# Softcap attention with a max-out layer behind it: a fourth step of the attention loop inverts its sums on chip, reciprocals are spread before the transposing DMA, turned reciprocals get buffers of their own, and GpSimd takes five of six weight differences

## The chip, the core and the metric

One core of a Trainium2 chip runs the whole kernel. TensorE (PE) multiplies matrices; VectorE (DVE), ScalarE (ACT) and GpSimd (POOL) do elementwise work; SyncE (SP) issues most of the DMAs, in program order, as does each engine with its own instructions. Matrix products land in PSUM, everything else on chip lies in SBUF. The metric is device time in microseconds (us), median over runs, from launch to end of one execution.

## The reference

`q`, `k`, `v` are 8 batches of 12 heads of 448 rows of 64; the weights `w1`, `w2` are 768x1024 and `w_out` is 1024x768.

```python
scores = scale * np.matmul(q, k.transpose(0, 1, 3, 2))
scores = cap * np.tanh(scores / cap)
scores = scores - np.max(scores, axis=-1, keepdims=True)
attn = np.exp(scores)
attn = attn / (np.sum(attn, axis=-1, keepdims=True) + 1e-09)
attn_out = np.matmul(attn, v)
...
x = attn_out.transpose(0, 2, 1, 3).reshape(B * S, H * D)
g = np.maximum(x @ w1, x @ w2)
out = g @ w_out
```

## The kernel before

**Algebra.** Since max(a, b) = b + relu(a - b), the kernel forms `wd = w1 - w2` (six slices of 128 rows, `subtract(c)`, L217) and `wm = w2 @ w_out` (`turn_w2`, `premultiply`) once, and then out = relu(x wd) w_out + x wm. No row maximum is taken, because tanh bounds the scores; the sum of the exponentials divides at the end.

**Steps.** Heads are handled in pairs, 48 of them; one step `t` (0 to 23) of the attention loop takes two pairs, `ab` = 0 and 1. Six pairs, or three steps, make one batch. Loads, casts and crossbar transposes go in groups `g` of three pairs: `load` (SP), `cast` (mostly GpSimd, to bf16), then for g >= 2 `cross(g)` (L271), a transposing DMA that writes `qkT`, which the score matmuls read. A step makes scores in four parts (L298, L293), ScalarE takes tanh (L299, L301) and exp (L306) of each, PE multiplies with the values (L341, L344; tile `pv`), and VectorE adds the exponentials up in `esum` (L325, L327, L329), so that few matmuls with ones give the row sums (`ss`). The score parts of step t+1 are issued during step t.

**Two ways to invert the sums.** Steps in the tuple `CHIP` (L513) do it on chip: `turn` transposes the sums in 32x32 blocks on VectorE (L385), `unturn` takes the reciprocal of one column (L389) and transposes it back (L391); for steps from 3 on (`chip_late`) GpSimd then multiplies pair 0 (L435) and VectorE pair 1 straight from PSUM (L438). All other steps go through DRAM: VectorE copies sums (L366) and values (L350), a DMA packs the sums (L368), VectorE inverts (`invert`, L396) in the next step, a DMA writes them out (L398), two DMAs broadcast them to all partitions (`spread`, L404, tile `rec_b`) in the step after that, and GpSimd multiplies both pairs (`normalize`, L418). Both ways write `xT`, the x of the reference.

**Filler.** The max-out layer of a batch (`moe(b)`: L455 multiplies by `wd`, L459 takes the relu, L467 and L470 multiply by `wm` and `w_out`, L474 copies out) is a queue of single matmuls, of which `F(n)` puts the next n between the matmuls of the attention. moe(0) is queued at the end of step 2, moe(1) at step 6, moe(2) at 9, moe(3) at 12, moe(4) at 17, and so on. So the order on PE is fixed by the program, and a matmul that waits holds up all behind it, scores too. What is left of the filler runs behind the attention loop.

**Order on the other queues.** In step t of the loop SP is given `cross(crosses[t])` (steps 4, 5, 7, 8, 10, 11, 13, 14, 16, 17, 19, 20), then `spread(t - 2)` where step t-2 is not in `CHIP`, then the loads; `normalize(t - 2)` is queued on GpSimd in the middle of the step.

**Buffers.** A pool hands out the buffers of a name in turn, and a new user waits until all readers of the old one are through: `tn` has two, shared by the turned sums and the turned reciprocals, `rec_b` has one, `w2T` three, `qkT` two.

Of the kernel before, what the change touches and what calls it, by code (L numbers as in the profile page):

```python
# [10 lines left out]
def kernel(  # L11
# [12 lines left out]
    f32 = mybir.dt.float32  # L24
    bf16 = mybir.dt.bfloat16
# [3 lines left out]
    B, H, S, D = q.shape  # L29
# [3 lines left out]
    P = 128  # L33
    KC, FC = DM // P, DF // P
# [13 lines left out]
    stage = ctx.enter_context(tc.tile_pool(name="stage", bufs=2))  # L48
    att = ctx.enter_context(tc.tile_pool(name="att", bufs=2))
    upool = ctx.enter_context(tc.tile_pool(name="upool", bufs=2))  # L50
    xpool = ctx.enter_context(tc.tile_pool(name="xpool", bufs=2))
# [164 lines left out]
    def subtract(c, eng=nc.vector):  # L216
        eng.tensor_sub(wd_sb[:, c, :], w1_in[c], w2b[:, c, :])  # L217

    w2T = {}

    def turn_w2(c):
        ps = mm_psum.tile([P, 512], f32, name="mm").bitcast(bf16)
        for f in range(FC):
            nc.tensor.transpose(ps[:, f * P : (f + 1) * P], w2b[:, c, f * P : (f + 1) * P], ident)
            yield
        w2T[c] = stage.tile([P, FC * P], bf16, name="w2T", bufs=3)
        nc.vector.tensor_copy(w2T[c], ps)

    def premultiply(c):
# [39 lines left out]
    def cross(g):  # L269

        nc.sync.dma_start_transpose(  # L271
            out=qkT_of(g).rearrange("p n j c -> p (n j) c"), in_=kqf[g % 2].rearrange("p n j c -> p (n j c)")
        )
# [6 lines left out]
    def scores(t, p, m0=0, m1=2):  # L280

        if m0 == 0:
            tanh[t, p] = att.tile([P, 4, S], bf16, name="tanh")
        if p == 2:
            s = s_psum.tile([P, 2, 512], f32, name="s")
        for m, (ab, j) in list(enumerate(PARTS[p]))[m0:m1]:
            i = 2 * t + ab
            g = i // L
            k0 = qkT[g][:, i % L, :, :].rearrange("p j c -> p (j c)")
            o = Q0 + (64 * (i // NP % 2) if g >= NT else 0)  # L290
            qTn = k0[:, o : o + S]
            if p == 2:
                nc.tensor.matmul(s[:, m, :S], k0[:, 3 * P : 4 * P], qTn)  # L293
                continue
            s = s_psum.tile([P, 2, 512], f32, name="s")
            for h in range(2):
                r = slice(64 * h, 64 * h + 64)
                nc.tensor.matmul(s[:, h, :S], k0[r, j * P : (j + 1) * P], qTn[r, :])  # L298
            nc.scalar.activation(tanh[t, p][:, 2 * m : 2 * m + 2, :], s[:, :, :S], AF.Tanh, scale=scale / cap)  # L299
        if p == 2:  # L300
            nc.scalar.activation(tanh[t, p][:, 0:2, :], s[:, :, :S], AF.Tanh, scale=scale / cap)  # L301

    def ex(t, p):
        n = 2 if p == 2 else 4
        expo[t, p] = att.tile([P, n, S], bf16, name=f"expo{p}", bufs=1 if p == 3 else 2)
        nc.scalar.activation(expo[t, p], tanh[t, p][:, 0:n, :], AF.Exp, scale=float(cap))  # L306

    def e_of(t, ab, j):
        p, m = LP[ab, j]
        return expo[t, p][:, m : m + (1 if j == NJ else 2), :]  # L310
# [20 lines left out]
    U, sums, rec, recd = {}, {}, {}, {}  # L331
    HALF = [slice(64 * h, 64 * h + 64) for h in range(2)]
    NB = S // 32
# [13 lines left out]
    def keep(t, ab, ps):  # L347
        if ab == 0:
            U[t] = upool.tile([P, 2, S], f32, name="u", bufs=3)
        nc.vector.tensor_copy(U[t][:, ab, :], ps[:, :S])  # L350
# [19 lines left out]
    turned = {}  # L370

    def turn(t, ab):

        ss = pv_psum.tile([P, 512], f32, name="ss")
        if t < NS:
            for j in range(NJ):
                for h in range(2):
                    nc.tensor.matmul(ss[HALF[h], :S], ones, e_of(t, ab, j)[:, h, :], start=(j == 0), stop=False)
            for h in range(2):
                nc.tensor.matmul(ss[HALF[h], :S], ones2[:, h, :], expo[t, 2][:, ab, :], start=False, stop=True)  # L380
        else:
            for h in range(2):
                nc.tensor.matmul(ss[HALF[h], :S], ones, esum[t][:, 2 * ab + h, :], start=True, stop=True)
        st = turned[t, ab] = upool.tile([P, NB, 32], f32, name="tn", bufs=2)
        nc.vector.transpose(st.rearrange("p b c -> p (b c)"), ss[:, :S])  # L385

    def unturn(t, ab):
        rs = upool.tile([P, NB, 1], f32, name="rs", bufs=2)
        nc.vector.reciprocal(rs, turned[t, ab][:, :, 0:1])  # L389
        rb = upool.tile([P, S], f32, name="tn", bufs=2)  # L390
        nc.vector.transpose(rb.rearrange("p (b c) -> p b c", c=32), rs.to_broadcast([P, NB, 32]))  # L391
        return rb

# [4 lines left out]
        nc.sync.dma_start(out=recd[t], in_=r)  # L398

    def spread(t):  # L400
        rec[t] = xpool.tile([P, 2, S], f32, name="rec_b", bufs=1)
        lines = recd[t].rearrange("(n h a) c -> h n (a c)", h=2, a=8)
        for h in range(2):
            nc.sync.dma_start(  # L404
                out=rec[t][64 * h : 64 * h + 64, :, :], in_=lines[h : h + 1, :, :].to_broadcast([64, 2, S])
            )
# [9 lines left out]
    def normalize(t):  # L416
        for ab in range(2):
            nc.gpsimd.tensor_mul(x_of(t, ab), U[t][:, ab, :], rec[t][:, ab, :])  # L418

    def chip(t, ab):  # L420
        turn(t, ab)
        ps = values(t, ab)
        yield
        rb = unturn(t, ab)
        yield
        nc.vector.tensor_mul(x_of(t, ab), ps[:, :S], rb)
# [13 lines left out]
    def run(parts, n=2):  # L440
        for _ in parts:
            F(n)
# [56 lines left out]
    def F(n):  # L499
        rate[1] += n * rate[0]  # L500
        while rate[1] >= 1 and fill_q:
            try:
                next(fill_q[0])
                rate[1] -= 1
            except StopIteration:
                fill_q.pop(0)
        if not fill_q:
            rate[1] = 0.0
# [1 line left out]

    NL = N // L
    NS = 3
    CHIP = (0, 1, 2, 4, 5, 8, 11)  # L513
    todo = [[] for _ in range(N)]
    crosses = {}

# [42 lines left out]
    for _ in turn_w2(0):  # L559
        pass  # L560
# [34 lines left out]
    def extra(i):  # L595
        for f, a in todo[i]:
            f(*a)
# [6 lines left out]
    for _ in turn_w2(1):  # L604
        pass
# [22 lines left out]
    for t in range(1, 3):  # L628
        scores(t + 1, 0)
        ex(t, 3)  # L630
        F(6)
        if t == 2:
            subtract(0)
        run(chip(t, 0), 5)
        if t == 2:
            for c in range(1, 5):
                subtract(c, nc.gpsimd)
            cast(nc.gpsimd, 3, "k")
            cast(nc.gpsimd, 3, "q")
            cross(3)  # L640
        F(6)
        scores(t + 1, 1)
        ex(t + 1, 0)
        F(6)
        run(chip(t, 1), 5)
        if t == 2:
            subtract(5)
            cast(nc.gpsimd, 2, "v")
            load(3, "v")
            fill_q.append(moe(0))  # L650
        scores(t + 1, 2)
        ex(t + 1, 1)
        F(10)
        if t == 2:
            extra(4)
            extra(5)
        scores(t + 1, 3)
        ex(t + 1, 2)
        F(8)
    add(3, 0, 0)  # L660

    for t in range(3, NQ):
        i = 2 * t
        more = t + 1 < NQ
        if t % 3 == 0 and 3 < t < 13 or t % 3 == 2 and t > 16:
            fill_q.append(moe(t // 3 - 1))
        if more:
            scores(t + 1, 0)
        ex(t, 3)
        F(2)  # L670
        add(t, 0, 1)
        F(6 if more else 2)
        if t in crosses:
            cross(crosses[t])
        if t > 4 and t - 2 not in CHIP:
            spread(t - 2)
        if t == 3:
            cast(nc.gpsimd, 3, "v")
        extra(i)
        F(5 if more else 3)  # L680
        if more:
            scores(t + 1, 1)
            ex(t + 1, 0)
        keep(t, 0, values(t, 0))
        F(4)
        add(t, 1, 0)
        F(6 if more else 4)
        if t > 4 and t - 2 not in CHIP:
            normalize(t - 2)
        if more:  # L690
            scores(t + 1, 2)
            ex(t + 1, 1)
        add(t, 0, 2)
        F(2)
        add(t, 1, 2)
        F(4 if more else 3)
        add(t, 1, 1)
        F(2 if more else 8)
        if t > 3 and t - 1 not in CHIP:
            invert(t - 1)  # L700
        extra(i + 1)
        F(2 if more else 0)
        if more:
            scores(t + 1, 3)
            ex(t + 1, 2)
        if t in CHIP:
            run(chip_late(t), 1)
        else:
            keep(t, 1, values(t, 1))
            total(t)  # L710
            F(3)
        F(1)
        if more:
            add(t + 1, 0, 0)
        F(3 if more else 0)
    F(6)
    spread(NQ - 2)
    F(10)
    invert(NQ - 1)
# [40 lines left out]
```

## Time and profile before

| what | value |
|---|---|
| median of 7 runs | 378.62 us |
| lowest, highest | 376.97, 382.16 us |
| the profiled execution | 381.26 us, of which the span is 379.5 us |
| PE busy | 348.1 us (92% of the span) |
| ScalarE busy | 281.5 us (74%) |
| VectorE busy | 247.7 us (65%) |
| GpSimd busy | 158.5 us (42%) |
| mean granted TensorE clock | 0.976 of full |

The span runs from the first instruction to the last; the 1.76 us between span and time lie around it. A timeline line gives the start, the duration, the engine, the line of the code, the operation, its output and input, a count, and in brackets the idle time ahead of it with what ended it. A line of the chain of waits gives start, duration and what the chain passed through. ScalarE works until 311.5 us; behind that only filler is left on PE.

### The profile page before, as it was taken

To read this page: it belongs to the slowest core of one execution; us is meant where nothing else is said; L and a number is where in the kernel's file an instruction comes from. 1 tells how busy PE (TensorE), PEld (TensorE's weight loads), DVE (VectorE), ACT (ScalarE), POOL (GpSimd) and SP (SyncE) were. 2 spreads that over 40 slices of the span, in tenths; PEclk is the share of its full clock that TensorE was granted. 3 is DMA by queue.
4 is the path that set the end of the run, shared out by engine and by line. 5 is a ranking of instruction groups with operands and counts; after the bars stand their busy time and mean duration, and the time that the engine had idled before them with its cause. 6 is when DMAs were issued, how large, how long until landed. Compare 5 with 4: busy or idle time off the path is not lost.

```text
span 379.5 us, 6115 instructions
## 1 busy us (share of the span) xinstructions
PE 348.1 (92%) x2278; PEld 165.9 (44%) x2278; DVE 247.7 (65%) x413; ACT 281.5 (74%) x265; POOL 158.5 (42%) x193
## 2 busy tenths in 40 slices
PE   4679988999599998899999999999999899999996
PEld 2335543444134443244444444444444345555553
DVE  4237647868747667877879758688676878433521
ACT  4993678999949997699999999999999892000000
POOL 6635782703374136611692266427734232220000
PEclk9899999999879998899999999999999999999999
DMA  7999969672984499387894987797985032322022
GB/s 254 260 224 301 328 190 245 197 197 63 261 259 89 127 255 287 118 153 206 259 257 149 265 251 212 207 286 208 206 222 159 2 92 92 115 95 99 2 83 85
DMA packets 109523, 69.80 MB, mean 184 GB/s; under 512 B 64308, under 2 KB 104500, under 8 KB 109492
## 3 DMA queue, kind: packets, MB, share of 16 engines
q1 hardware_dynamic: 107540, 66.25, 62.4%
q0 software_dynamic: 1952, 3.15, 4.5%
q8 instruction: 18, 0.29, 0.3%
q14 instruction: 13, 0.11, 0.1%
HBM read 50.27 MB, written 11.13 MB: 162 GB/s over the span
## 4 chain that ended last, share of the span: by engine, by line
PE 34%; ACT 30%; DMA 12%; SPq 8%; POOL 6%; issue 5%; DVE 5%; POOLq 0%; DVEq 0%; ACTq 0%
ACT expo L306 14%; ACT tanh L299 13%; PE mm L455 11%; PE mm L470 9%; PE mm L467 7%; DMA qr<-in_q_dram 5%; PE pv L341 3%; DMA vr<-in_v_dram 3%; DMA kr<-in_k_dram 2%; DMA rec_b<-rec_d 2%; PE s L298 2%; SPq L271 2%; ACT tanh L301 2%; SPq L131 2%; POOL xT L418 1%
## 5 line engine op out<-in xcount | busy, mean ns | idle before, releaser
L299 ACT ACTIVATE tanh<-s 128x896 bf16<-128x896 f32 x144 | 124.2, 914 | 29.9 <-PE s L298 28.1
L306 ACT ACTIVATE expo<-tanh 128x1792 bf16<-128x1792 bf16 (+1 forms) x96 | 144.8, 1509 | 0.1
L470 PE MATMUL mm<-wo_sb,gT 128*128 128x384 bf16 x448 | 87.6, 330 | 0.0
L455 PE MATMUL mm<-xT,wd_sb 128*128 128x448 bf16 x384 | 81.9, 362 | 4.9 <-POOL xT L418 3.0
L418 POOL TENSOR_TENSOR xT<-u,rec_b 128x448 bf16<-128x448 f32 x34 | 41.2, 1233 | 92.5 <-DMA rec_b<-rec_d 62.5
L467 PE MATMUL mm<-wm_sb,xT 128*128 128x384 bf16 x336 | 69.4, 329 | 3.4 <-DVE osb L474 1.8
L470 PEld LDWEIGHTS <-gT 128*128 128x128 bf16 x448 | 43.2, 99 | 31.5 <-issue 4.9
L298 PE MATMUL s<-qkT 64*128 64x448 bf16 x288 | 45.9, 366 | 11.2 <-ACT tanh L299 5.5
L455 PEld LDWEIGHTS <-wd_sb 128*128 128x128 bf16 x384 | 37.0, 99 | 43.1 <-issue 10.8
L474 DVE COPY osb<-mm 128x384 f32<-128x384 f32 x56 | 30.9, 552 | 32.3 <-PE mm L470 32.1
L459 DVE TENSOR_SCALAR gT<-mm 128x448 bf16<-128x448 f32 x64 | 39.6, 618 | 18.5 <-PE mm L455 18.4
L350 DVE COPY u<-pv 128x448 f32<-128x448 f32 x38 | 23.5, 619 | 37.7 <-PE pv L344 35.8
L467 PEld LDWEIGHTS <-xT 128*128 128x128 bf16 x336 | 32.3, 98 | 24.1 <-issue 4.1
L159 POOL CAST vp<-vr 128x1152 bf16<-128x1152 f32 x14 | 16.5, 1181 | 49.5 <-DMA vr<-in_v_dram 30.8
L341 PE MATMUL pv<-expo,vp 128*64 128x448 bf16 x288 | 36.3, 360 | 0.0
L329 DVE TENSOR_TENSOR esum<-esum,expo 128x896 bf16<-128x896 bf16 x42 | 34.3, 817 | 2.4
L325 DVE TENSOR_TENSOR esum<-esum,expo 64x896 bf16<-64x896 bf16 x42 | 33.4, 796 | 0.8
L327 DVE TENSOR_TENSOR esum<-expo 128x896 bf16<-128x896 bf16 x42 | 33.4, 796 | 0.0
L298 PEld LDWEIGHTS <-qkT 64*128 64x128 bf16 x288 | 12.1, 94 | 45.9 <-issue 43.3
L301 ACT ACTIVATE tanh<-s 128x896 bf16<-128x896 f32 x24 | 22.0, 916 | 3.5 <-PE s L293 2.6
L179 POOL CAST kqf<-kr 128x1152 bf16<-128x1152 f32 x14 | 18.2, 1301 | 6.8 <-DMA kr<-in_k_dram 6.5
L341 PEld LDWEIGHTS <-vp 128*64 128x64 bf16 x288 | 13.1, 109 | 16.7 <-issue 11.9
(74 smaller groups left out, 265.2 us busy)
## 6 DMA issues: line engine op xcount, KB each, us to landing
kr<-in_k_dram SPq DMA_DIRECT2D x14, 576.0 KB, 5.5
qr<-in_q_dram SPq DMA_DIRECT2D x14, 576.0 KB, 6.9
vr<-in_v_dram SPq DMA_DIRECT2D x14, 576.0 KB, 4.5
out_dram<-osb SPq DMA_DIRECT2D x20, 384.0 KB, 3.6
rec_b<-rec_d SPq DMA_DIRECT2D x34, 224.0 KB, 3.6
out_dram<-osb SPq DMA_DIRECT2D x16, 192.0 KB, 3.2
osb<-in_moe_w_dram SPq DMA_DIRECT2D x4, 512.0 KB
gT<-in_moe_w_dram POOLq DMA_DIRECT2D x6, 256.0 KB, 12.4
```

What stands on the lines that cost most here:

```text
L298: nc.tensor.matmul(s[:, h, :S], k0[r, j * P : (j + 1) * P], qTn[r, :])
L299: nc.scalar.activation(tanh[t, p][:, 2 * m : 2 * m + 2, :], s[:, :, :S], AF.Tanh, scale=scale / cap)
L306: nc.scalar.activation(expo[t, p], tanh[t, p][:, 0:n, :], AF.Exp, scale=float(cap))
L325: nc.vector.tensor_add(d, d, expo[t, 2][r, :, :])
L327: nc.vector.tensor_add(d, e_of(t, ab, 1 if ab else 0), e_of(t, ab, 2 if ab else 1))
L329: nc.vector.tensor_add(d, d, e_of(t, ab, 0 if ab else 2))
L341: nc.tensor.matmul(ps[HALF[h], :S], vp[g % 2][:, 2 * n + h, j, :], e_of(t, ab, j)[:, h, :], start=(j == 0), stop=False)
L418: nc.gpsimd.tensor_mul(x_of(t, ab), U[t][:, ab, :], rec[t][:, ab, :])
L455: nc.tensor.matmul(ps[:, :S], wd_sb[:, c, f * P : (f + 1) * P], x[:, c, cs], start=(c == 0), stop=(c == KC - 1))
L459: nc.vector.tensor_relu(g[:, f, cs], ps[:, :S])
L467: nc.tensor.matmul(ps[:, : DM // 2], x[:, c, ts], wm_sb[:, c, hs], start=(c == 0), stop=False)
L470: nc.tensor.matmul(ps[:, : DM // 2], g[:, f, ts], wo_sb[:, f, hs], start=False, stop=(f == FC - 1))
```

## The change

```diff
-        w2T[c] = stage.tile([P, FC * P], bf16, name="w2T", bufs=3)
+        w2T[c] = stage.tile([P, FC * P], bf16, name="w2T", bufs=2)
...
-        st = turned[t, ab] = upool.tile([P, NB, 32], f32, name="tn", bufs=2)
+        st = turned[t, ab] = upool.tile([P, NB, 32], f32, name="tn", bufs=1)
...
-        rb = upool.tile([P, S], f32, name="tn", bufs=2)
+        rb = upool.tile([P, S], f32, name="rb", bufs=2)
...
-        rec[t] = xpool.tile([P, 2, S], f32, name="rec_b", bufs=1)
+        rec[t] = xpool.tile([P, 2, S], f32, name="rec_b", bufs=2)
...
-    CHIP = (0, 1, 2, 4, 5, 8, 11)
+    CHIP = (0, 1, 2, 3, 4, 5, 8, 11)
...
         if t == 2:
-            for c in range(1, 5):
+            for c in range(1, KC):
                 subtract(c, nc.gpsimd)
             cast(nc.gpsimd, 3, "k")
...
         if t == 2:
-            subtract(5)
             cast(nc.gpsimd, 2, "v")
...
+        if t > 4 and t - 2 not in CHIP:
+            spread(t - 2)
         if t in crosses:
             cross(crosses[t])
-        if t > 4 and t - 2 not in CHIP:
-            spread(t - 2)
```

Step 3 joins the steps that invert on chip. The turned sums (`tn`) keep one buffer, the turned reciprocals (`rb`) get two of their own, `rec_b` gets a second, `w2T` gives one up. The last slice of `w1 - w2`, c = 5, goes from VectorE to GpSimd, where it follows slices 1 to 4 and stands ahead of the casts of group 3. In the steps that have both, the two broadcast DMAs are issued before the transposing DMA; these are steps 8, 11, 14, 16, 17, 19 and 20.

## The prediction

> **What bounds the kernel now.** I read the busy shares first: PE is busy for 348.1 of 379.5 us, ScalarE for 281.5. The timeline of ScalarE then shows that from 171.4 us to 298 us it has no gap over 0.1 us: a step takes 11.8 us there, set by tanh and exp. Behind its end at 311.5 us PE runs a fixed rest of filler, about 68 us with almost no gap. Since the filler is dealt out by count, that rest does not depend on how the loop went. So time is lost, for good, wherever ScalarE waits inside the loop. Its gaps over 0.8 us behind 60 us are these five:
>
> ```profile
> 62.72 1.73 ACT L299 ACTIVATE tanh<-s 128x896 bf16<-128x896 f32 x2 [1.55 <-PE s L298]
> 109.24 1.73 ACT L299 ACTIVATE tanh<-s 128x896 bf16<-128x896 f32 x2 [5.20 <-PE s L298]
> 145.88 1.73 ACT L299 ACTIVATE tanh<-s 128x896 bf16<-128x896 f32 x2 [0.82 <-PE s L298]
> 150.69 0.92 ACT L301 ACTIVATE tanh<-s 128x896 bf16<-128x896 f32 x1 [1.50 <-PE s L293]
> 158.76 1.73 ACT L299 ACTIVATE tanh<-s 128x896 bf16<-128x896 f32 x2 [2.98 <-PE s L298]
> ```
>
> Each waits for scores, so PE was late. The timeline of PE says why; the bracket names what ended its idle time:
>
> ```profile
> 61.20 1.12 PE L455 MATMUL mm<-xT,wd_sb 128*128 128x448 bf16 x5 [1.69 <-DVE wd_sb L217]
> 99.92 0.37 PE L298 MATMUL s<-qkT 64*128 64x448 bf16 x2 [0.44 <-ACT tanh L299]
> 102.35 0.53 PE L455 MATMUL mm<-xT,wd_sb 128*128 128x448 bf16 x1 [2.06 <-POOL xT L418]
> 103.82 1.28 PE L455 MATMUL mm<-xT,wd_sb 128*128 128x448 bf16 x3 [0.94 <-POOL xT L418]
> 105.29 3.52 PE L455 MATMUL mm<-xT,wd_sb 128*128 128x448 bf16 x9 [0.19 <-POOL xT L435]
> 145.16 0.32 PE L467 MATMUL mm<-wm_sb,xT 128*128 128x384 bf16 x1 [1.81 <-DVE osb L474]
> 155.87 0.36 PE L362 MATMUL ss<-esum,ones 128*32 128x448 bf16 x2 [1.89 <-DVE esum L329]
> ```
>
> The third to fifth are the start of moe(1), which needs x of steps 3, 4 and 5. The chain of waits leads there through SP:
>
> ```profile
> 92.64 3.40 SPq L271
> ...
> 96.13 0.64 SPq L404
> ...
> 96.82 4.18 DMA rec_b<-rec_d
> ...
> 101.16 2.60 POOL xT L418 x2
> 103.76 1.48 POOL xT L435
> ```
>
> The transpose of group 5 is issued, then the broadcast of step 3's reciprocals, then GpSimd multiplies step 3 and only then pair 0 of step 5, although the latter's reciprocals were ready at 98.9 (L391). The cost does not end with the gap. The table by stretches grants PE a clock of 0.50 from 102 to 108 us (0.79 to 110), and the nine matmuls at 105.29 take 0.39 us apiece, against 0.19 (1.89 for ten) at full clock. The same follows the gaps at 145.16 (0.60 and 0.55 from 146 to 150) and 155.87 (0.66 and 0.50 from 156 to 160).
>
> Behind those two gaps stand these lines of VectorE and GpSimd:
>
> ```profile
> 142.81 0.65 DVE L391 STREAM_TRANSPOSE tn<-rs 128x448 f32<-128x448 f32 x1 [2.06 <-POOL xT L435]
> 151.70 4.11 DVE L329 TENSOR_TENSOR esum<-esum,expo 128x896 bf16<-128x896 bf16 x1
> 152.03 2.21 POOL L418 TENSOR_TENSOR xT<-u,rec_b 128x448 bf16<-128x448 f32 x2
> ```
>
> **Part by part.**
>
> *Step 3 on chip.* It takes step 3's two L418 multiplies (2.60 us), its sums, reciprocal and broadcast DMAs off SP, and the wait for them off GpSimd. x(3,0) and x(3,1) are then ready near 79 us. At step 5 GpSimd is free from 90.4, so pair 0's multiply (1.14 us) ends at about 100.1, and pair 1's on VectorE at 100.91 + 0.62 = 101.5. PE comes to moe(1) at 100.3, does four matmuls of steps 3 and 4 and one of step 5 (5 x 0.19, to 101.25), and waits some 0.3 us for the sixth: too short, beside the 1.69 us at 61.20 after which the clock stayed at 1.00, to expect a lower clock. The 13 filler matmuls ahead of the next scores end at 100.3 + 13 x 0.19 + 0.3 = 103.1; ScalarE runs dry at 104.04. So all of its 5.20 us goes.
> It adds, in step 3, on VectorE four block transposes (4 x 0.65), two reciprocals (2 x 0.24) and a multiply (0.62), 3.7 us, less two copies (2 x 0.61) and a reciprocal (0.48), so 2.0 us net, near 75 to 79 us. Covers: VectorE idles 2.34 us at 80.5; values of step 4 need `pv` at 79.40, and the last reader ends at 75.08 + 3.7 = 78.8. Bounds: 0 to 2.0 us of ScalarE time if the cover fails; I take 0.4, near the cover. PE's matmul count does not change (4 L362 for 4 L383). One more L435 on GpSimd (1.14) precedes group 5's casts, which ended at 76.4; their reader, the transpose at 92.64, leaves 16 us.
>
> *Own buffers for turned reciprocals.* L391 at 142.81 waited 2.06 us because its buffer was still read by L435, which stood behind step 6's broadcast. That put the copy L474 at 144.56 and PE at 145.16. Without it the copy ends at 144.56 + 0.55 - 2.06 = 143.05, before PE's need at 143.35: the gap, the slow clock behind it and ScalarE's 0.82 + 1.50 = 2.32 us go. What is late next is VectorE's add L329 (below).
>
> *GpSimd takes slice 5.* PE's need of it (58.41 + 5 x 0.19 = 59.5) is then met only by x(2,1), which L426 writes at 59.39 + 0.62 = 60.0, in place of 61.15: 1.15 us gained. GpSimd pays 2.13 us (mean 2.129 of L217 there; VectorE paid 1.217) at about 50 us, and pushes group 3's casts, its transpose on SP (55.45) and the loads queued behind it by as much. The transpose would be issued by 57.6 + 3.11 and land 5.3 us later (median of its kind, counted from the issue's end, the later reading): 66.0, against its reader, the second score part at 67.41 - 1.15 = 66.3. Bounds 0 to 2.1 us; as the median still fits, I take 0.3.
>
> *Broadcast ahead of the transpose, second `rec_b`, `w2T` of two.* Only the start of moe(1) ever waited for L418, and that is gone, so the earlier multiply frees nothing but GpSimd, whose 62.5 us of waiting for `rec_b` cost nothing else. The second buffer frees SP of one 2.2 us wait for L418, behind which loads stood that nobody missed. `w2T` costs nothing: the copy of slice c+2 waits for its own transposes, which PE runs behind `premultiply(c)`, the last reader of the old buffer. The transposes come 1.3 us later (two issues), plus up to 1.8 us where SP must wait for the written reciprocals (longest such wait before). Their readers leave: in step 19 it was issued until 264.92 + 4.13, lands 5.3 later by 274.4, and is read some 0.5 ahead of the next step's first tanh (277.60), near 277.1; in step 16 it lands by 238.6 and is read near 241.7: 2.7 us or more. I take 0.
>
> *The starved add.* L329 at 151.70 took 4.11 us, against 0.61 to 0.63 mostly, while GpSimd ran without pause from 145.7 to 158.5. Of the 2.98 + 0.44 us lost behind it, nothing in the change removes the cause; it moves VectorE 2 us against GpSimd's burst. Bounds: 0 to 3.42 gained, or as much lost elsewhere. Other bursts (185 to 199, 220 to 234, 257 to 271) slowed adds to 1.4 to 2.2 us and opened no gap on PE, so I take half the gain, 1.7.
>
> The page "SBUF — State Buffer" of the Trainium skill (section "SBUF: two separate sides") speaks against this change: a VectorE operation with two SBUF inputs and a GpSimd one exclude each other for a whole instruction. The trace's 4.11 us beside an unbroken run of GpSimd agrees; by the rule alone the two added GpSimd operations could each hold VectorE up for their length, 2.13 + 1.14 = 3.3 us, leaving a gain of 6.1. The page "TensorE: Matmul & The Clock Gate" (Part 1) puts the drop of the clock after an idle window of about 3.4 us; here it fell after gaps of 1.81 and 1.89 us, and the trace decides. By the rule the slow stretch at 146 to 150 had another cause and its 1.50 us would stay, leaving a gain of 7.9.
>
> **Sum** against the profiled execution: 5.20 + 2.32 + 1.15 + 1.70 = 10.4; less 0.3 (sixth matmul at moe(1)), 0.4 and 0.3 from above: 9.4. 381.26 - 9.4 = 371.9. That execution stands 2.64 us above the median. If this excess is the starved add, which other runs then lacked, the median gains 9.4 - 1.7 = 7.7 and lands at 370.9; if it lies elsewhere, 378.62 - 9.4 = 369.2. I take 370.
>
> **Rivals.** *GpSimd starves VectorE elsewhere.* A denser schedule meets the same bursts; each starved add that a sum matmul needs costs 3.4 us (above), two leave 9.4 - 6.8 = 2.6: 376; one leaves 373. For it: `ss` at step 6 was issued the moment the add ended (115.87); against: one case in the whole trace.
> *PE cannot use the time.* If PE's own load sets the pace, gaps close in one place and open later. For it: 8.00 of 8 us busy in many stretches. A step with its 40 filler matmuls all of L455 costs 40 x 0.19 + 4.2 (scores 1.8, values 2.0, sums 0.4, by the chain's pieces near 110 to 122 us) = 11.8, all of ScalarE's 11.8, and ScalarE lost 0.37 in such a step at 118. Against: from 171 on PE keeps up. It would leave slice 5 and half of the rest, or nothing: 374 to 378.
> *Late transposes, slower.* In seven steps the transposing DMA comes later; from 2.7 us (even groups, steps 16 and 19) to some 6 us (odd groups, read one part later) on, scores and so ScalarE wait. To end 1% slower, 9.4 + 3.8 = 13.2 us must be lost, 1.9 us past the margin in each: 4.6 to 8 us of delay, against 1.3 + 1.8 = 3.1 worked out. Then 383 to 386.
> That a part does not happen is excluded: the built program has the instructions moved as described.
>
> **How the numbers follow.** Forecast 0.69 (366 to 373), starving 0.13, PE-bound 0.11, late transposes 0.07. Low end: all gains without debits are 12.1 from 378.62, so 366.5, and 365 with the 1.55 and 0.3 us rests of ScalarE's gaps; high end 376, with starving twice. A measurement here tells about 1% (3.8 us) from no change. Faster by more: the forecast, most of starving, little of PE-bound, 0.82; same 0.11; slower 0.07.
>
> **What would show it.** In the changed profile: no gap of ScalarE near 104 and no clock below 0.8 there; L391 never waiting for L435; L455 near 60 us waiting for VectorE's L426, not L217; ScalarE's last instruction ending some 9 us before 311.5, and the rest behind it still 68 us. I am wrong if ScalarE's gaps turn up with `qkT` as the late tile, if adds of 2 us and more are followed by sum matmuls, or if PE shows new idle time over 1.7 us.

## The result and the profile after

The changed kernel takes 376.95 us (median of 26 runs, 374.99 to 378.25), the kernel before 379.88 us (63 runs on the same chips, 376.91 to 384.04). The ratio is 0.9924, 95% interval [0.9907, 0.9941]: 2.9 us gained, where 8.6 were forecast, and 0.95 us above the top of the range, 376. The profiled execution of the changed kernel took 375.6 us, with a span of 373.8 and a clock of 0.995. Its span is 5.7 us shorter than that of before, more than the medians show: the profiled execution of before stands 1.4 us above its median, that of after 1.35 below.

The page's busy shares after, one line for all engines (busy us, share of the span, instructions), and the granted clock in 40 slices:

```profile
span 373.8 us, 6110 instructions
...
PE 346.2 (93%) x2278; PEld 165.0 (44%) x2278; DVE 248.6 (67%) x416; ACT 281.5 (75%) x265; POOL 162.1 (43%) x193
...
PEclk9999999999999999899999999999999999999999
```

The work is nearly that of before. One slice is still below 9: the 17th, at 149.5 to 158.9 us. The timeline of ScalarE after shows what lies there:

```profile
61.73 1.73 ACT L299 ACTIVATE tanh<-s 128x896 bf16<-128x896 f32 x2 [0.40 <-PE s L298]
...
103.21 1.73 ACT L299 ACTIVATE tanh<-s 128x896 bf16<-128x896 f32 x2 [0.16 <-PE s L298]
...
112.48 1.73 ACT L299 ACTIVATE tanh<-s 128x896 bf16<-128x896 f32 x2 [0.64 <-PE s L298]
...
155.24 1.73 ACT L299 ACTIVATE tanh<-s 128x896 bf16<-128x896 f32 x2 [3.82 <-PE s L298]
...
159.30 0.92 ACT L301 ACTIVATE tanh<-s 128x896 bf16<-128x896 f32 x1 [0.75 <-PE s L293]
...
293.47 1.73 ACT L299 ACTIVATE tanh<-s 128x896 bf16<-128x896 f32 x2 [0.94 <-PE s L298]
...
307.31 2.54 ACT L306 ACTIVATE expo<-tanh 128x896 bf16<-128x896 bf16 x2
```

The waits of 1.55, 5.20, 0.82, 1.50 and 2.98 us of before are down to 0.40, 0.16 and nothing. The tanh that started at 158.76 before starts at 148.11 after: 10.65 us earlier. The very next one waits 3.82 us, at the start of moe(2). From there to the end of the loop ScalarE waits 3.82 + 0.75 + 0.30 + 0.61 + 0.94 + 0.45 = 6.87 us, where before it waited 0.44 + 0.30 + 0.68 + 0.45 = 1.87. So 5.0 us are given back, 4.1 of them at moe(2), and some 5.7 stay, which is the difference of the spans.

The timeline of PE after, the matmuls with `wd`:

```profile
60.23 1.11 PE L455 MATMUL mm<-xT,wd_sb 128*128 128x448 bf16 x5 [0.55 <-DVE xT L426]
...
100.67 1.48 PE L455 MATMUL mm<-xT,wd_sb 128*128 128x448 bf16 x7 [0.32 <-DVE xT L438]
...
147.60 0.55 PE L455 MATMUL mm<-xT,wd_sb 128*128 128x448 bf16 x2
150.74 0.35 PE L455 MATMUL mm<-xT,wd_sb 128*128 128x448 bf16 x1 [2.59 <-POOL xT L418]
151.83 2.83 PE L455 MATMUL mm<-xT,wd_sb 128*128 128x448 bf16 x10 [0.74 <-POOL xT L418]
```

moe(1), at 100.67, waits 0.32 us. moe(2), at 147.60, does two matmuls and then waits for GpSimd's L418, which multiplies step 7. Before, moe(2) began at 158.96 and found that multiply done: it ended at 152.03 + 2.21 = 154.24, 4.72 us earlier. After, PE comes 11.36 us earlier, but the multiply only 2.47 (it ends at 149.56 + 2.21 = 151.77): 11.36 - 2.47 - 4.72 = 4.2 us are missing. The chain of waits after shows why the multiply does not come sooner:

```profile
136.46 5.49 DMA rec_d<-rec_s
142.01 3.38 DMA rec_b<-rec_d
145.44 1.15 POOL kqf L179
146.59 0.69 POOL kqf L191
147.73 1.42 POOL kqf L179
149.56 2.22 POOL xT L418 x2
151.83 2.83 PE mm L455 x10
```

The reciprocals of step 7 are written at 136.46, spread by 145.4, and GpSimd then still has casts to do. Its timeline has the casts in front of the multiply:

```profile
143.54 1.14 POOL L159 CAST vp<-vr 128x1152 bf16<-128x1152 f32 x1 [7.83 <-PE s L298]
...
145.44 1.15 POOL L179 CAST kqf<-kr 128x1152 bf16<-128x1152 f32 x1
...
147.73 1.42 POOL L179 CAST kqf<-qr 128x1152 bf16<-128x1152 f32 x1
...
149.56 2.21 POOL L418 TENSOR_TENSOR xT<-u,rec_b 128x448 bf16<-128x448 f32 x2
```

GpSimd is idle for 7.83 us ahead of the cast of `v`. The multiply could not have run there, since its own input, the broadcast, is not due before 145.4; but the casts then run from 143.54 to 149.56, 6.0 us, and the multiply is queued behind them. It starts 4.2 us after its input is there, which are the 4.2 us that are missing. (The bracket names PE, whose scores do not feed this cast; a run below names the load of `v`.) SP's timeline shows that load behind the transposing DMA and the loads of `k` and `q`, and the broadcast waiting for the written reciprocals:

```profile
126.84 5.54 SPq L271 DMA_TRANSPOSE qkT<-kqf  x1
...
136.46 0.37 SPq L398 DMA_DIRECT2D rec_d<-rec_s  x1
136.92 0.40 SPq L126 DMA_DIRECT2D vr<-in_v_dram  x1
137.37 2.05 SPq L137 DMA_DIRECT2D vr<-in_v_dram  x2
142.01 1.23 SPq L404 DMA_DIRECT2D rec_b<-rec_d  x2
```

As at moe(1) before, the gap costs more than its length, as the table by stretches of 2 us after shows (the stretch and its length, busy us of PE, PEld, DVE, ACT and POOL, then clock, DMA share, GB/s):

```profile
152.00:154.00 2.00, 2.00 (x9) 0.93 (x8) 0.62 (x1) 0.00 (x0) 1.88 (x4) 0.74 1.30 148
154.00:156.00 2.00, 2.00 (x10) 0.50 (x10) 0.62 (x1) 0.76 (x1) 1.21 (x2) 0.50 1.31 295
156.00:158.00 2.00, 2.00 (x14) 0.80 (x10) 0.96 (x2) 2.00 (x3) 0.00 (x0) 0.91 0.88 236
```

PE is busy in all three, at a clock of 0.74, 0.50 and 0.91.

### The profile page after: what moved, and what is told of

Its sections match the earlier page's. It is cut to its first block, busy times and chain, and to the rows that moved or that the text cites. A ratio compares the mean times of both kernels' runs of the same rounds, so it can differ in the third digit from the quotient of the medians.

```text
span 373.8 us, 6110 instructions
## 1 busy us (share of the span) xinstructions
PE 346.2 (93%) x2278; PEld 165.0 (44%) x2278; DVE 248.6 (67%) x416; ACT 281.5 (75%) x265; POOL 162.1 (43%) x193
## 4 chain that ended last, share of the span: by engine, by line
PE 49%; ACT 28%; DVE 13%; POOL 4%; DMA 3%; issue 2%; SPq 0%; DVEq 0%; POOLq 0%; ACTq 0%
ACT expo L306 13%; ACT tanh L299 13%; PE mm L455 11%; PE mm L470 10%; PE mm L467 8%; PE s L298 5%; PE pv L341 4%; PE mm L235 3%; DVE esum L327 3%; ACT tanh L301 3%; DVE esum L325 2%; PE pv L344 2%; DVE gT L459 2%; DMA rec_d<-rec_s 1%; POOL kqf L179 1%
## 5 line engine op out<-in xcount | busy, mean ns | idle before, releaser
L470 PE MATMUL mm<-wo_sb,gT 128*128 128x384 bf16 x448 | 86.4, 326 | 0.0
L455 PE MATMUL mm<-xT,wd_sb 128*128 128x448 bf16 x384 | 80.7, 355 | 5.1 <-POOL xT L418 3.3
L418 POOL TENSOR_TENSOR xT<-u,rec_b 128x448 bf16<-128x448 f32 x32 | 40.6, 1288 | 62.2 <-DMA rec_b<-rec_d 49.1
L455 PEld LDWEIGHTS <-wd_sb 128*128 128x128 bf16 x384 | 36.5, 98 | 41.6 <-issue 11.0
L474 DVE COPY osb<-mm 128x384 f32<-128x384 f32 x56 | 30.9, 551 | 32.2 <-PE mm L470 32.0
L350 DVE COPY u<-pv 128x448 f32<-128x448 f32 x37 | 22.6, 612 | 35.5 <-PE pv L344 32.6
L325 DVE TENSOR_TENSOR esum<-esum,expo 64x896 bf16<-64x896 bf16 x42 | 35.5, 845 | 0.8
L327 DVE TENSOR_TENSOR esum<-expo 128x896 bf16<-128x896 bf16 x42 | 34.1, 811 | 0.0
L329 DVE TENSOR_TENSOR esum<-esum,expo 128x896 bf16<-128x896 bf16 x42 | 32.0, 762 | 2.4
L298 PEld LDWEIGHTS <-qkT 64*128 64x128 bf16 x288 | 11.3, 95 | 42.0 <-issue 39.4
```

The source lines that it names most:

```text
L325: nc.vector.tensor_add(d, d, expo[t, 2][r, :, :])
L327: nc.vector.tensor_add(d, e_of(t, ab, 1 if ab else 0), e_of(t, ab, 2 if ab else 1))
L455: nc.tensor.matmul(ps[:, :S], wd_sb[:, c, f * P : (f + 1) * P], x[:, c, cs], start=(c == 0), stop=(c == KC - 1))
L470: nc.tensor.matmul(ps[:, : DM // 2], g[:, f, ts], wo_sb[:, f, hs], start=False, stop=(f == FC - 1))
```

## The experiments

**The theory** to test: the gain arrives as summed, and 4 us of it go back at moe(2), because GpSimd's multiply of step 7 stayed where it was. **The rivals:** PE has no time to spare, so that a gap closed in one place opens in another whatever GpSimd does; or a part of the change costs time by itself. A further question was which part earns what, since the chain showed that two of them could each end the wait at moe(1). All times are medians, those of before from the same chip.

*The changed kernel once more*, to see whether the gap is of the kernel or of one execution.

> The changed kernel as it is, as a control beside the others on this chip and for a second trace. Theory (the gain at moe(1) is given back at moe(2), because x of step 7 comes late from GpSimd): ratio to before near 0.992, and again an idle PE of 2 to 4 us ended by POOL xT L418 near 147 to 152 us, with ScalarE waiting 3 to 5 us behind it. Rival (that gap was an accident of one execution): no such gap, and the lost time in another place.

375.22 us against 379.64, ratio 0.9897 [0.9859, 0.9935]. PE's timeline has the gap again:

```profile
151.10 0.35 PE L455 MATMUL mm<-xT,wd_sb 128*128 128x448 bf16 x1 [3.05 <-POOL xT L418]
```

ScalarE waits 4.85 us behind it. The gap belongs to the kernel.

*Step 7 on chip too*, so that nothing of moe(2) hangs on the broadcast of step 7 or on the casts:

```diff
-    CHIP = (0, 1, 2, 3, 4, 5, 8, 11)
+    CHIP = (0, 1, 2, 3, 4, 5, 7, 8, 11)
```

> The changed kernel with step 7 inverted on chip as well, so that moe(2) needs no L418 of step 7. Theory: the gap of PE at 147 to 152 us, the clock under 1.0 behind it and ScalarE's 3.82 + 0.75 us of waiting go; time 3 to 4.5 us under the changed kernel, ratio to before 0.980 to 0.985. Rival (PE and ScalarE have no slack left there, or VectorE's added 2 us come due): time equal to the changed kernel within 1.5 us, the waiting found elsewhere, for example at sum matmuls behind slow adds.

371.0 us (370.5 to 371.95) against 379.64, ratio 0.9781 [0.9744, 0.9818]. PE's timeline at the start of moe(2):

```profile
148.97 2.63 PE L455 MATMUL mm<-xT,wd_sb 128*128 128x448 bf16 x13
```

Thirteen matmuls run without a wait, at full clock (2.63 / 13 = 0.20 us apiece). Against the changed kernel on the same chip this is 375.22 - 371.0 = 4.2 us, the 4.1 that the trace showed as given back. That PE had no time to spare is refuted: it takes the 4 us as soon as its input is there.

*The multiply ahead of the casts*, with step 7 still through DRAM: this moves nothing but the order on GpSimd.

```diff
+        if t == 9:
+            normalize(7)
         extra(i)
...
-        if t > 4 and t - 2 not in CHIP:
+        if t > 4 and t != 9 and t - 2 not in CHIP:
```

> The changed kernel with GpSimd's multiply of step 7 queued ahead of step 9's casts (v of group 7, k and q of group 8). Theory A (x of step 7 is late because it stands behind 6 us of casts, which wait for the load of v): the multiply ends near 149 us, the gap of PE at moe(2) shrinks from 3.3 us to under 1 us and the time falls by 1 to 3.5 us, less if the casts, now 2 to 4 us later, make the transpose of group 8 and the scores of step 11 late. Theory B (the broadcast of step 7's reciprocals lands late by itself, near 147 us): the multiply ends at most 1 us earlier and the time stays within 1 us of the changed kernel.

373.07 us (372.09 to 373.53) against 379.5, ratio 0.9834 [0.9806, 0.9862]. GpSimd's timeline:

```profile
147.70 2.60 POOL L418 TENSOR_TENSOR xT<-u,rec_b 128x448 bf16<-128x448 f32 x2 [11.23 <-DMA rec_b<-rec_d]
150.25 1.14 POOL L159 CAST vp<-vr 128x1152 bf16<-128x1152 f32 x1
```

and PE's:

```profile
150.36 2.05 PE L455 MATMUL mm<-xT,wd_sb 128*128 128x448 bf16 x10 [1.12 <-POOL xT L418]
```

The multiply now waits for its own input, the broadcast, and not for the casts. One wait of 1.12 us is left, and the ten matmuls behind it run at full clock. ScalarE waits 0.63 us at moe(2), where the changed kernel has 3.82 + 0.75; waits of 0.56, 0.64 and 0.84 us follow, the last at 175.23. By the ratios, 0.9897 for the changed kernel when it ran once more and 0.9781 with step 7 on chip, the order of these casts alone carries somewhat more than half of what was given back. The broadcast, which is there only at 147.70 here, carries a part; how the rest divides is open.

*Step 3 off chip again.*

```diff
-    CHIP = (0, 1, 2, 3, 4, 5, 8, 11)
+    CHIP = (0, 1, 2, 4, 5, 8, 11)
```

> The changed kernel with step 3 taken back off the on-chip steps. Theory: the wait at moe(1) returns (PE waits 2 to 4 us for POOL xT L418 near 100 us, ScalarE 4 to 6 us), but moe(2) is then reached later and its wait shrinks or goes, so the time is only 1 to 3 us above the changed kernel (ratio to before 0.993 to 1.000). Rival (step 3 was worth its 5.2 us for itself, and the loss at moe(2) has nothing to do with it): 5 us above the changed kernel, ratio about 1.005, with the gap at moe(2) still there.

375.73 us against 379.64, ratio 0.9898 [0.9864, 0.9933]: as the changed kernel on that chip (375.22). Without step 3 the wait at moe(1) should have come back by the prediction. GpSimd's timeline shows that it does not:

```profile
96.78 2.23 POOL L418 TENSOR_TENSOR xT<-u,rec_b 128x448 bf16<-128x448 f32 x2 [6.45 <-DMA rec_b<-rec_d]
98.96 1.13 POOL L435 TENSOR_TENSOR xT<-u,rb 128x448 bf16<-128x448 f32 x1
```

The multiply of step 3 stood at 101.16 to 103.76 in the kernel before. With the broadcast issued ahead of the transpose it ends at 99.0, and PE waits 0.33 us at moe(1). I had given the 5.20 us to step 3 on chip and nothing to the broadcast, and either (the next run has step 3 alone) does all or most of it.

*The order back, step 3 still on chip:* `cross` ahead of `spread`, all else as in the changed kernel.

```diff
-        if t > 4 and t - 2 not in CHIP:
-            spread(t - 2)
         if t in crosses:
             cross(crosses[t])
+        if t > 4 and t - 2 not in CHIP:
+            spread(t - 2)
```

> The changed kernel with the transposing DMA ahead of the broadcasts again. Theory (step 3 on chip and the earlier broadcast each suffice to free the start of moe(1), and the own buffers keep VectorE from waiting at step 8): no gap at moe(1), the gap at moe(2) stays at 2 to 4 us, time within 1.5 us of the changed kernel. Rival (the earlier broadcast alone carries the gain at steps 5 and 8): PE waits again near 137 us, and the time rises by 2 us or more.

374.99 us (six runs, 371.67 to 377.62) against 379.38, ratio 0.9854 [0.9799, 0.9908]. moe(1) waits 0.30 us, moe(2) still 2.06 + 0.74 (in a profiled execution that was the longest of the six, at a mean clock of 0.948; the median of the other five is 374.57). So the wait at moe(1) ends without the new order too, if step 3 is on chip. Whether this is faster than the changed kernel stays open with that spread.

*Both back:* that order, and step 3 off chip.

> The changed kernel with the transposing DMA first again and step 3 off the chip, so that both remedies of moe(1) are gone; slice 5 on GpSimd and the own buffers stay. Theory: the wait at moe(1) is back in full (POOL xT L418 near 100 us, 4 to 5 us of ScalarE), the wait at moe(2) is smaller than 1.5 us or gone; in sum 1 to 3 us above the changed kernel (377 to 379.5). Rival (the parts add up): the wait at moe(1) is back and the one at moe(2) stays, 5 us above.

377.88 us (12 runs) against 379.38, ratio 0.9951 [0.9915, 0.9987]. PE's timeline has the start of moe(1) as it was before:

```profile
101.97 0.35 PE L455 MATMUL mm<-xT,wd_sb 128*128 128x448 bf16 x1 [1.67 <-POOL xT L418]
...
103.44 0.93 PE L455 MATMUL mm<-xT,wd_sb 128*128 128x448 bf16 x3 [1.12 <-POOL xT L418]
104.91 3.00 PE L455 MATMUL mm<-xT,wd_sb 128*128 128x448 bf16 x9 [0.54 <-POOL xT L435]
```

ScalarE waits 4.24 us behind that. At moe(2) 1.08 + 0.74 us are left of PE's gap, and 2.98 us of ScalarE's wait, which is more than the 1.5 that I expected at most, and less than the 3.82 + 0.75 of the changed kernel. It is the seesaw of the theory: of what moe(1) keeps, moe(2) has less to give back. Against the kernel with step 3 on chip and the same order, on the same chip, this one is 377.88 - 374.99 = 2.9 us slower (3.3 against the other five executions of that one), and 0.9 against the median of the changed kernel on all chips: ending a wait of 4 to 5 us at moe(1) is worth 1 to 3 us.

*Turned sums and reciprocals in one pair of buffers again.*

```diff
-        st = turned[t, ab] = upool.tile([P, NB, 32], f32, name="tn", bufs=1)
+        st = turned[t, ab] = upool.tile([P, NB, 32], f32, name="tn", bufs=2)
...
-        rb = upool.tile([P, S], f32, name="rb", bufs=2)
+        rb = upool.tile([P, S], f32, name="tn", bufs=2)
```

> The changed kernel with turned sums and turned reciprocals sharing two buffers again, as before. Theory: L391 of step 8 again waits for L435, but the earlier broadcast (ahead of the transpose) has taken most of that wait away, and what is lost there only shortens the wait at moe(2): within 1.5 us of the changed kernel. Rival (the prediction's step): the gap at PE near 137 us and the slow clock behind it return, and the time rises by 2.3 us, ratio about 0.998.

376.54 us (12 runs) against 379.64, ratio 0.9934 [0.9905, 0.9962]. PE waits 0.19 us for L474 at 137.61, where before it waited 1.81, and 2.96 us at moe(2). With the broadcast ahead of the transpose, GpSimd's L435 is early enough that L391 waits only 0.44 us for it (at 135.26), where it waited 2.06, so the own buffers too mostly do a thing that another part has done already. On the same chip this is 1.3 us above the changed kernel (375.22), and the two intervals overlap.

*Slice 5 of the weight difference on VectorE again* (`range(1, 5)`, and `subtract(5)` where it was).

> The changed kernel with slice 5 of w1 - w2 on VectorE again. Theory: PE waits 1.7 us for it near 60 us, all behind comes 1.2 us later, and the wait at moe(2), which hangs on loads and casts that come no later, shrinks by as much: within 0.6 us of the changed kernel. Rival (the prediction's step): the full 1.2 us slower, the gap at moe(2) unchanged.

376.59 us (12 runs) against 379.38, ratio 0.9917 [0.9885, 0.9949]: as the changed kernel. ScalarE's first wait is 1.55 us again. The gap at moe(2) did not shrink, as PE's timeline shows:

```profile
153.00 0.53 PE L455 MATMUL mm<-xT,wd_sb 128*128 128x448 bf16 x1 [3.77 <-POOL xT L418]
```

GpSimd's timeline has the cast of `v` waiting by name for its load:

```profile
145.62 1.14 POOL L159 CAST vp<-vr 128x1152 bf16<-128x1152 f32 x1 [8.83 <-DMA vr<-in_v_dram]
...
151.82 2.21 POOL L418 TENSOR_TENSOR xT<-u,rec_b 128x448 bf16<-128x448 f32 x2
```

Both lines are 2.1 to 2.3 us later than in the changed kernel, more than PE's work moved. Why this load landed so late is open. That the time is the same agrees with the 1.15 us of slice 5 being gained and given back, but this run doesn't show how.

*The broadcast first, alone*, on the kernel before (with the second `rec_b` and two `w2T`):

```diff
-    name="rec_b", bufs=1
+    name="rec_b", bufs=2
...
+        if t > 4 and t - 2 not in CHIP:
+            spread(t - 2)
         if t in crosses:
             cross(crosses[t])
-        if t > 4 and t - 2 not in CHIP:
-            spread(t - 2)
```

> The kernel before with the broadcasts ahead of the transpose as the only edit (two buffers for them, two of w2T for room). Theory (this part, priced at nothing in the prediction, carries nearly all of the gain, and what it frees is given back at moe(2) in part): no wait of PE for L418 over 1 us near 100 us, VectorE's L391 at step 8 waiting under 0.5 us, a gap of 1 to 4 us at moe(2); time within 1.5 us of the changed kernel, ratio 0.990 to 0.997. Rival (step 3 on chip or own buffers carry it): ratio 0.997 or more, with the old gaps.

377.75 us (12 runs) against 379.5, ratio 0.9956 [0.9927, 0.9984]. Of the wait at moe(1) 0.20 + 0.99 us are left, L391 waits 0.44 us, and ScalarE loses 6.06 us at moe(2). The part that I priced at nothing removes most of moe(1)'s wait by itself, and its gain goes back in the same place.

*The same with step 7 on chip* (7 added to `CHIP`, 3 not).

> The kernel before with only two edits: broadcasts ahead of the transpose (with two buffers for them, and two of w2T for room), and step 7 on chip in place of step 3. Slice 5 stays with VectorE, the turned tiles share two buffers. Theory: moe(1) and moe(2) both start without waiting; only the 1.2 us at slice 5 is missed: 371 to 373 us, ratio 0.978 to 0.983. Rival (step 3 on chip or the own buffers are needed for it): a wait at moe(1) or at step 8 shows, and the time is 374 or more.

372.22 us (371.28 to 373.51) against 379.38, ratio 0.980 [0.976, 0.9839]. moe(2) has no gap. One step of the attention moved to the chip turns a gain of 1.75 us into one of 7.2.

*And with slice 5 on GpSimd besides*: three parts, without step 3 on chip and without own buffers.

> The kernel before with three edits: broadcasts ahead of the transpose, slice 5 of w1 - w2 on GpSimd, and step 7 on chip. Step 3 stays off the chip and the turned tiles share two buffers. Theory (once moe(2) starts without waiting, slice 5 is worth its 1.2 us, and step 3 on chip and the own buffers are worth nothing): 370.5 to 371.5 us, as the changed kernel with step 7 added (371.0). Rival (slice 5's gain is swallowed by a later wait, or step 3 and the own buffers are worth a part of the 1.2 us): 372 us or more, as with slice 5 on VectorE.

371.21 us (370.09 to 372.95) against 378.43, ratio 0.9802 [0.9751, 0.9852]; no wait of PE reaches 1 us between 60 and 285 us. This and the changed kernel with step 7 on chip are some 2% below the kernel before, and the latter, on the same chip, 1.1% below the changed kernel (371.0 against 375.22). Between the two the runs show no difference (0.9802 and 0.9781, with intervals of 0.004 to 0.005 to each side), so whatever step 3 on chip and own buffers still earn once step 7 is on chip is too small to show in these times. The traces leave room for it: ScalarE waits 0.84 us at moe(1) here, 0.16 there.

*The kernel before once more*, for the add of 4.11 us.

> The kernel before, for a second trace. Theory (the add of 4.11 us at 151.7 us was an accident of the profiled execution, and 1 to 3 us of its time with it): ScalarE's wait near 109 us of about 5 us is there again, the waits between 144 and 160 us sum to less than 4 us, against 5.7 before. Rival (all of it is the kernel's own): the same three waits within 0.5 us.

380.06 us, span 378.2. ScalarE waits 4.93, 1.21, 1.50 and 1.33 us at the places of the 5.20, 0.82, 1.50 and 2.98. VectorE in the same place, by its timeline:

```profile
152.45 0.72 DVE L329 TENSOR_TENSOR esum<-esum,expo 128x896 bf16<-128x896 bf16 x1
...
155.54 3.24 DVE L327 TENSOR_TENSOR esum<-expo 128x896 bf16<-128x896 bf16 x1
158.71 0.54 DVE L474 COPY osb<-mm 128x384 f32<-128x384 f32 x1
159.18 0.69 DVE L329 TENSOR_TENSOR esum<-esum,expo 128x896 bf16<-128x896 bf16 x1
```

and PE behind it:

```profile
159.31 1.50 PE L455 MATMUL mm<-xT,wd_sb 128*128 128x448 bf16 x7 [1.31 <-DVE osb L474]
```

The add of 4.11 us takes 0.72 here. But another add, L327, takes 3.24 us beside the same two multiplies of GpSimd (L418, from 155.00), the copy L474 stands behind it, PE waits for the copy, and ScalarE waits 1.33 us for PE. So a slow add in this place belongs to the kernel, and only which add it is, and what hangs on it, is of one execution: 2.98 + 0.44 us in the first profile, 1.33 in the second. The three waits sum to 1.21 + 1.50 + 1.33 = 4.04, about the 4 us that I expected at most.

## Why the prediction was wrong, point by point

**The step that failed** is in the part on the broadcast: "Only the start of moe(1) ever waited for L418, and that is gone, so the earlier multiply frees nothing but GpSimd". It was true of the kernel before, and said nothing of a kernel in which PE comes 9 us earlier. With it went the premise that "time is lost, for good, wherever ScalarE waits inside the loop": a wait removed is gained only up to the slack of the next input that PE needs. That slack was in the trace: L418 at 152.03 + 2.21, a line which the prediction shows for another reason, against moe(2) at 158.96, so 4.72 us, and the sum was 9.4. Behind the waits near 145 us I asked what is late next on VectorE, and not on GpSimd. The runs showed in its place: PE came to moe(2) 11.36 us earlier and L418 of step 7, behind the casts, only 2.47, so that PE waited 2.59 + 0.74 us for it. The gain up to that place was mis-sized by little (10.65 us measured against 9.4); the 4.1 us given back there are most of the error. With step 7 on chip, where moe(2) does not wait, the time is 371.0, within the forecast's own 366 to 373.

**The terms of the sum.** Slice 5: 1.55 to 0.40 us of ScalarE's time, the 1.15 predicted, and L455 at 60.23 waits for L426 as foretold. moe(1): 5.20 to 0.16, as predicted in size, and the remaining 0.32 us of PE are the "some 0.3" of the sixth matmul. But the cause was put to step 3 on chip alone, and the runs without it show the broadcast doing the same. Own buffers: the 2.32 us went, and again they go without them, once the broadcast is first. The starved add: gone from this place, but not by anything that the sum counted. The second profile of before has a slow add there too, at a lower price (1.33 us against 2.98 + 0.44), so that the half was near the mark by luck. After, the same multiplies run while PE waits at moe(2) and VectorE has little to do (0.14 us busy from 148 to 152), and the slow adds stand elsewhere: L327 at 222.50 (4.13 us) and L325 at 229.28 (3.00 us), each beside such a pair of multiplies. The debits for VectorE in step 3 and for group 3's transpose did not show as waits of scores at their places; 0.64 us at 112.48 and 0.25 at 116.03 are new, against 0.37 at 118.14 before. In the range, the low end of 365 counts 1.15 us twice: of ScalarE's 1.55 only 0.40 is not yet in the 12.1.

**A misreading that cost nothing.** The text has ScalarE end at 311.5 us with 68 us of filler behind. That is where its last tanh starts. The last line of its timeline in the kernel before:

```profile
313.10 2.54 ACT L306 ACTIVATE expo<-tanh 128x896 bf16<-128x896 bf16 x2
```

It ends at 315.64, and the rest is 379.5 - 315.64 = 63.86 us. After, it is 373.8 - 307.31 - 2.54 = 63.95: the fixed rest, on which the whole sum hangs, holds to a tenth.

**The rivals.** Starved adds: they came, at a small price. Behind the 3.00 us add, sum matmuls wait 0.43 and 0.31 us (233.45 and 234.11) and ScalarE 0.61 (236.12), against 3.4 us apiece as priced; the 4.13 us add set off no wait of ScalarE. PE's own load as the pace: refuted by the run with step 7 on chip, though its outward sign, gaps that open later, is just what appeared; it was the input that was late, not PE that was full. Late transposes: they did take longer (median 3.74 us against 3.20 of the time that SP is held, by the rows of the tile `qkT`), and SP waited 14.0 us in seven waits for written reciprocals ahead of a broadcast, the longest 3.1, against the 1.8 that I took. But no score waited for a transposing DMA. To put this term at nothing was still not worked out: the text's own delay of 3.1 us is more than its margin of 2.7. A mixed case, in which the gain comes and half of it goes back at the next moe, was not among them.

**The signs.** No gap near 104, full clock there, L391 never behind L435, L455 behind L426: all four seen. That ScalarE would end some 9 us earlier was not: it ends 5.8 us earlier (309.85 against 315.64). Of the signs against me two came: "new idle time over 1.7 us" on PE, the 2.59 us ahead of 150.74, and an add of over 2 us followed by sum matmuls that wait, for the 0.43 and 0.31 us above.

## What to carry to other kernels

A removed wait brings work forward only as far as the next input allows, so before a sum is made, look up for every later meeting point of the engines how long its last producer had been done (here 4.7 us), and whether the change moves that producer too. When several edits aim at one wait, undo them singly: here either of two removed most of the same 5 us, and the sum by parts credited one of them alone. The place where a gain goes back can be the cheapest next edit: on one chip the whole change gave 379.64 - 375.22 = 4.4 us and step 7 on chip another 4.2, and the multiply ahead of the casts alone gave somewhat over half of that.

## What the runs showed of the hardware

The clock fell after shorter idle times of PE than I would have thought. It stood at 0.50 in a stretch behind a single gap of 2.19 us (second profile of before) and behind 2.59 + 0.74 us (after); the prediction had 1.81 and 1.89 us, and 1.69 us without effect. With both remedies of moe(1) taken back it stood at 0.50 (156 to 158 us) behind two gaps of 1.08 and 0.74 us at moe(2); with the multiply ahead of the casts, a single gap of 1.12 us there left it at 1.00. The page "TensorE: Matmul & The Clock Gate" of the Trainium skill (Part 1) puts the drop after an idle window of about 3.4 us; no single gap of these reaches that, so the measurement decides.

A VectorE add that meets a pair of GpSimd multiplies (L418) can take several times its 0.6 us: in each of the 14 traces the longest add, of 2.1 to 4.1 us, overlaps such a pair. Which add it is varies between executions of the same program (4.11 us for one add of before, 0.72 for the same add in the second profile, where the next takes 3.24), so a price from one trace is here one draw. The rule of the page "SBUF — State Buffer" (section "SBUF: two separate sides"), by which such operations exclude each other, allows for the slow adds. That the two GpSimd operations added by this change would hold VectorE up for 3.3 us is not borne out: beside slice 5 VectorE's own slice takes 1.60 us where it took 1.22, and between 61 and 100 us PE has no wait for VectorE.
